# Longformer attention and squared-ReLU expert on one core: batch 1's global rows by one-hot matmuls, and expert matmuls placed ahead of the last scatter

## The chip, the cores and the metric

The kernel runs on one core of one Trainium2 chip. The metric is the device time of one execution in microseconds (us); lower is better. The profile page describes one profiled execution of the same program. Its span is about 2 us shorter than the time of that execution, so spans are compared with spans and times with times.

Every comparison below is a ratio to the kernel before, measured in the same rounds on the same chip, or a distance between two events inside one trace. Where absolute times of different runs are compared all the same, the text says so.

## The reference, cut to what matters

```python
# q, k, v: 8 batches x 8 heads x 576 tokens x 64; global_idx: 8 sorted token numbers
scores = np.matmul(q, k.transpose(0, 1, 3, 2)) / np.sqrt(D)
mask = np.abs(pos[:, None] - pos[None, :]) <= 32              # a window of 65
mask = mask | is_global[:, None] | is_global[None, :]         # 8 global tokens
attn = softmax(np.where(mask, scores, -1e9))
x = np.matmul(attn, v)          # -> (4608 tokens, 512)
h = x @ w_in                    # 512 -> 2048
out = np.square(np.maximum(h, 0)) @ w_out                     # -> (4608, 512) float32
```

The eight global tokens attend to everything and are attended to by everything. So their q, k and v rows are needed beside the windowed ones, and their results must be put into their columns of x ("scatter").

## The kernel before

The kernel works on pairs of heads: pair `i` is batch `i // 4`, heads `2*(i % 4)` and the next. Pairs 0 to 3 are batch 0, pairs 4 to 7 are batch 1. Attention runs on all engines: TensorE (PE) for scores and values, ScalarE (ACT) for exponentials, VectorE (DVE) for casts, copies and normalising, GpSimd (POOL) for the scatter. The expert's matmuls are "fills": blocks that are put between the attention steps to keep PE busy. `mm1` is the first expert matmul (`w_in`), `mm2` the output matmul (`w_out`). A score group covers half of a pair's tokens.

The names in the traces: `stk`, `stq`, `stv` are loaded rows of k, q, v; `natk`, `natq`, `vt` the same in fp16; `kt`, `qt` the transposed ones; `sc` the scores, `et` their exponentials, `acc` the sums of values, `xT` the attention's result, `gx` that of the global tokens; `rl` and `gt` are the expert's relu and its square; `gst` holds gathered rows, `gscr` is the scratch tensor in HBM. `sc`, `acc`, `tr` and `mm` are the buffers in PSUM that this kernel's matmuls write.

Batch 0 picks its global rows with one-hot matmuls (`oh`, `ohp`). All later batches get them by an indirect DMA (gather), a store to a scratch tensor in HBM, and small DMAs from there:

```python
bufs_of = {"sc": 1, "acc": 1, "tr": 1, "mm": 3}       # PSUM buffers by tag

def fetch_globals(b, hp):                              # per pair: 4 + 1 small DMAs
    for nm in "kq":
        js = range(TJ) if b == 1 else (TJ - 1,)
        for h in range(2):
            dst = st[nm][TP : TP + NG, 2 * hp + h, js[0] : TJ]
            nc.sync.dma_start(out=dst, in_=rows(nm)[:, h].unsqueeze(1).to_broadcast(...))
    nc.sync.dma_start(out=st["v"][0:NG, ...], in_=rows("v")...)

def transposed(nm, i):
    nat = nats.pop((nm, i))
    tr = pst("tr" if b else "mm", [P, 1024], FP16)     # k and q of b > 0 share one buffer
    for j in range(TJ):
        n = TP + NG if (b and j == TJ - 1) else TP
        nc.tensor.transpose(tr[:, TP * j : TP * j + n], nat[0:n, j, :], identity[0:n, 0:n])
    if b == 0:                                          # one-hot pick of the global rows
        gl = tr.bitcast(FP32)[:, 384 : 384 + NG]
        for j in range(TJ):
            nc.tensor.matmul(gl, nat[0:TP, j, :], ohp[0:TP, j, :], ...)
```

The part around batch 0's end and batch 1's start, in program order (`...` marks cuts):

```python
    for i in range(4): pool.dma_start(out=w_in[...], ...)     # 4 x 512 KB
    gs0 = gather_rows(0)                                       # POOL: 3 indirect DMAs
    for i in range(NHP):                                       # batch 0, first half
        et = scores(i, 0); ...; pv(*prev); keep_warm(1)
    pv(*prev)
    scatter(0, 0)                                              # 8 POOL copies of 4 pairs
    gather_store(0, gs0)
    ...                                                        # k, q, v of pair 4, its globals
    for j in range(4): pool.dma_start(out=w_out[...], ...)
    for i in range(NHP):                                       # batch 0, second half
        et = scores(i, 1)
        if i == 0: keep_warm(5)                                # idle matmuls
        if prev is not None: pv(*prev)
        fill(2 * step + 1, 2.5)
    pv(*prev); scatter(0, 1); gs1 = gather_rows(1); ...
    casts(NHP, 0); casts(NHP, 1, nc.vector.tensor_copy)        # natk, natq, values of pair 4
    take(2)                                                    # two expert blocks
    tr_k(NHP)
    while fills[0][0] < 16: take(1)
    tr_q(NHP)
    et0 = scores(NHP, 0)                                       # first scores of batch 1
```

`keep_warm(n)` is n matmuls of zeros whose result nobody reads. In `pv`, `acc` has a single buffer, which comes free when `xT` has been written from it.

The softmax here doesn't subtract the row's maximum and nothing guards it: scores larger than these inputs give would overflow.

## Time and profile before

The time before was 373.61 us (median of 3, 373.07 to 373.63).

| What | Value | View |
|---|---|---|
| PE busy | 347.7 of 370.9 us (94%) | page, busy times |
| First expert matmul | 28.91 us | timeline |
| PE waits for batch 1's first k, then q | 3.29 and 1.86 us | timeline |
| First scores of batch 1 | 49.54 us | timeline |
| First output matmul (w_out) | 60.87 us | timeline |
| First expert matmul behind batch 1's last scatter | 89.23 us | timeline |
| Granted clock (share of PE's full clock) 0.50 | 44 to 53.9 us | stretches |

The page of the kernel before: busy times, and the span in 40 slices of 9.3 us with PE's busy share and its granted clock in tenths (9 is 90% or more).

```profile
span 370.9 us, 8149 instructions
PE 347.7 (94%) x2878; PEld 184.8 (50%) x2878; DVE 249.2 (67%) x649; ACT 248.8 (67%) x479; POOL 54.0 (15%) x141
PE   7779689997999999999999999999999999999995
PEclk9978859999999999999999999999999999999999
```

PE is nearly full from the seventh slice on, apart from the tenth. What is to be won lies in the first 60 us.

The timeline of the kernel before. Columns: start and duration in us, engine, source line, operation, output<-inputs, shape, count; in brackets the idle time of that engine ahead of it and what ended it.

```profile
28.91 1.52 PE L475 MATMUL mm<-xT,w_in 128*128 128x256 f16 x8 [0.48 <-POOL xT L646]
42.97 0.56 DVE L386 CAST natk<-stk 104x768 f16<-104x768 f32 x1 [3.10 <-DMA stk<-gscr_k_691]
43.59 0.67 PE L415 MATMUL tr<-identity,natk 96*128 96x96 f16 x6 [3.29 <-DVE natk L386]
45.11 0.56 DVE L394 CAST vt_82<-stv 128x512 f16<-128x512 f32 x2 [1.58 <-DMA stv<-gscr_v_695]
46.78 0.65 DVE L431 COPY kt_72<-tr 128x480 f16<-128x480 f16 x1
47.83 0.65 PE L415 MATMUL tr<-identity,natq 96*128 96x96 f16 x6 [1.86 <-DVE kt_72 L438]
49.54 0.58 PE L557 MATMUL sc<-qt_77,kt_72 64*128 64x160 f16 x10 [0.31 <-DVE qt_77 L450]
50.05 3.60 PE L475 MATMUL mm<-xT,w_in 128*128 128x256 f16 x16
60.87 1.03 PE L496 MATMUL mm<-w_out,gt 128*128 128x512 f16 x4
```

Read it backwards from the first scores of batch 1 (49.54): they waited for qt, qt for the q transpose (47.83), that for the copies out of the one `tr` buffer (46.78). These copies stood in DVE's queue behind the cast of v at 45.11, for which DVE had waited 1.58 us, until the gathered rows of v (`gscr_v`) had landed. The train begins with the cast of natk at 42.97, which DVE did at once when the gathered rows of k (`gscr_k`) had landed. The gather had been issued at 21.97 us, so 21 us lie between it and the cast.

The same stretch as busy times of the kernel before. Columns: stretch, length, then for PE, weight loads, DVE, ACT, POOL the busy us (instructions), then granted clock, DMA share, GB/s.

```profile
40.00:42.00 2.00, 0.30 (x3) 0.02 (x1) 0.00 (x0) 0.00 (x0) 0.46 (x3) 1.00 1.01 136
44.00:46.00 2.00, 1.96 (x12) 1.11 (x9) 0.61 (x3) 1.41 (x3) 1.70 (x2) 0.50 1.24 208
```

After PE had stood still for 3.29 us, its granted clock was 0.50 until 53.9 us: the 16 expert matmuls at 50.05 took 3.60 us, and the 16 at 55.01, at a granted clock of 1.00, took 1.92 us.

### The profile page before, as it was taken

Reading aid. Unit: us, or ns where it says so; the run is one execution under the profiler, and the core shown is the slowest. Engines: PE = TensorE matmul, PEld = TensorE weight load, DVE = VectorE, ACT = ScalarE, POOL = GpSimd, SP = SyncE. Lnnn points to the kernel's source line nnn. Section 1 sums busy time; section 2 is a strip of 40 time slices with the busy share of each in tenths; the row PEclk is TensorE's granted clock in tenths of the full one; section 3 lists DMA queues with packets and bytes.
Section 4 is the critical chain, followed back from the end, with each engine's and each line's share of the span. In section 5 each row is a group of like instructions: output and inputs, shape, how many; then the busy total and the mean of one; then the engine's idle time right before and its main releaser. Section 6 shows DMA issues by size and latency. Waiting matters only on the chain.

```text
span 370.9 us, 8149 instructions
## 1 busy us (share of the span) xinstructions
PE 347.7 (94%) x2878; PEld 184.8 (50%) x2878; DVE 249.2 (67%) x649; ACT 248.8 (67%) x479; POOL 54.0 (15%) x141
## 2 busy tenths in 40 slices
PE   7779689997999999999999999999999999999995
PEld 3546456553545555555555555555555544444442
DVE  7652447566788988788878887888788863422421
ACT  6656336565997799769976997699769952612610
POOL 5375520004200340020002000200020001000000
PEclk9978859999999999999999999999999999999999
DMA  8899997769774574355435633562010002002002
GB/s 204 181 153 197 174 224 166 169 159 222 194 188 129 129 191 118 97 156 160 100 97 157 159 101 97 156 160 67 30 60 29 2 28 85 1 28 85 2 31 82
DMA packets 65650, 44.22 MB, mean 119 GB/s; under 512 B 43114, under 2 KB 60618, under 8 KB 65610
## 3 DMA queue, kind: packets, MB, share of 16 engines
q1 hardware_dynamic: 60200, 38.14, 39.8%
q0 software_dynamic: 4992, 4.98, 8.0%
q10 hardware_dynamic: 418, 0.59, 0.6%
q8 instruction: 22, 0.36, 0.4%
q14 instruction: 18, 0.15, 0.1%
HBM read 38.06 MB, written 9.83 MB: 129 GB/s over the span
## 4 chain that ended last, share of the span: by engine, by line
PE 59%; issue 15%; DMA 9%; DVE 6%; ACT 5%; POOL 3%; POOLq 1%; SPq 1%; ACTq 0%; DVEq 0%
PE mm L496 25%; PE mm L460 23%; DMA stv<-in_v_dram 4%; PE acc L595 4%; PE tr L415 3%; PE sc L557 3%; DMA gstq<-in_q_dram,gidx 3%; ACT rl L465 2%; DMA gstk<-in_k_dram,gidx 2%; DVE gt L466 2%; ACT er L563 1%; POOL xT L646 1%; POOLq L637 1%; DVE et L567 1%; ACT natq L386 1%
## 5 line engine op out<-in xcount | busy, mean ns | idle before, releaser
L496 PE MATMUL mm<-w_out,gt 128*128 128x512 f16 x576 | 133.7, 379 | 0.0
L460 PE MATMUL mm<-xT,w_in 128*128 128x512 f16 x512 | 119.0, 379 | 1.0 <-POOL xT L646 1.0
L465 ACT ACTIVATE rl<-mm 128x512 f16<-128x512 f32 x128 | 72.1, 594 | 33.0 <-PE mm L460 32.2
L496 PEld LDWEIGHTS <-gt 128*128 128x128 f16 x576 | 53.3, 97 | 55.4
L460 PEld LDWEIGHTS <-w_in 128*128 128x128 f16 x512 | 47.3, 97 | 50.3 <-issue 1.3
L605 ACT ACTIVATE rec<-acc 64x288 f32<-64x288 f32 (+1 forms) x112 | 45.4, 405 | 32.0 <-PE acc L595 25.5
L618 DVE TENSOR_TENSOR xT<-acc,rec 64x288 f16<-64x288 f32 (+1 forms) x112 | 50.8, 454 | 19.2 <-ACT rec L606 17.9
L466 DVE TENSOR_TENSOR gt<-rl 128x512 f16<-128x512 f16 x128 | 50.1, 421 | 16.6 <-ACT rl L465 15.8
L646 POOL COPY xT<-gx 128x4 f16 x72 | 19.8, 275 | 228.7 <-DVE xT L618 220.5
L563 ACT ACTIVATE er<-sc 128x912 f16<-128x912 f32 (+1 forms) x48 | 44.0, 916 | 5.5 <-PE sc L557 5.0
L567 DVE TENSOR_TENSOR et<-er,mask 128x912 f16<-128x912 f16 (+1 forms) x48 | 29.9, 622 | 21.3 <-ACT er L563 20.9
L502 DVE COPY ot<-mm 128x512 f32<-128x512 f32 x36 | 24.9, 691 | 26.0 <-PE mm L496 25.3
L386 ACT CAST natq<-stq 104x768 f16<-104x768 f32 (+1 forms) x32 | 26.4, 825 | 9.4 <-DMA stv<-gscr_v_695 5.2
L606 ACT ACTIVATE rec<-rec 128x288 f32<-128x288 f32 x64 | 28.3, 443 | 2.0
L563 ACT ACTIVATE et<-sc 128x912 f16<-128x912 f32 (+1 forms) x16 | 14.6, 913 | 14.5 <-PE sc L557 14.3
L386 DVE CAST natk<-stk 104x768 f16<-104x768 f32 (+1 forms) x32 | 17.8, 555 | 3.4 <-DMA stk<-gscr_k_691 3.1
L475 PE MATMUL mm<-xT,w_in 128*128 128x256 f16 x128 | 18.6, 306 | 0.5 <-POOL xT L646 0.5
L415 PE MATMUL tr<-identity,natk 96*128 96x96 f16 x168 | 12.4, 212 | 4.6 <-DVE natk L386 4.5
L415 PE MATMUL tr<-identity,natq 96*128 96x96 f16 x168 | 12.4, 211 | 3.6 <-DVE kt_72 L438 2.1
L475 PEld LDWEIGHTS <-w_in 128*128 128x128 f16 x128 | 13.3, 109 | 4.3 <-issue 1.0
L610 DVE TENSOR_REDUCE gs<-acc 128x16 f32<-128x32 f32 x32 | 6.0, 187 | 11.9 <-ACT rec L605 11.9
L415 PEld LDWEIGHTS <-natq 96*128 96x128 f16 x192 | 9.3, 99 | 9.1 <-issue 2.6
(195 smaller groups left out, 317.6 us busy)
## 6 DMA issues: line engine op xcount, KB each, us to landing
stk<-in_k_dram SPq DMA_DIRECT2D x32, 288.0 KB
out_dram<-ot SPq DMA_DIRECT2D x36, 256.0 KB
stq<-in_q_dram SPq DMA_DIRECT2D x30, 288.0 KB
stv<-in_v_dram SPq DMA_DIRECT2D x64, 120.0 KB
w_in<-in_moe_w_in_dram POOLq DMA_DIRECT2D x4, 512.0 KB, 9.0
w_out<-in_moe_w_out_dram POOLq DMA_DIRECT2D x4, 512.0 KB, 9.3
stv<-in_v_dram SPq DMA_DIRECT2D x32, 48.0 KB
stq<-in_q_dram ACTq DMA_DIRECT2D x2, 288.0 KB
```

The lines of the kernel that those rows point to most:

```text
L386: op(out=nat[0:n].rearrange("p j (h d) -> p h j d", d=D), in_=st[nm][0:n, 2 * hp : 2 * hp + 2],)
L415: nc.tensor.transpose(tr[:, TP * j : TP * j + n], nat[0:n, j, :], identity[0:n, 0:n])
L460: nc.tensor.matmul(ph, w_in[:, t, u * P : (u + 1) * P], xT[:, t, XOFF + c * TC : XOFF + (c + 1) * TC], start=(t == 0), stop=(t == NDM - 1),)
L465: nc.scalar.activation(out=rl, in_=ph, func=AF.Relu)
L466: nc.vector.tensor_tensor(out=gts[c][:, u, :], in0=rl, in1=rl, op=ALU.mult)
L475: nc.tensor.matmul(ph[:, j], w_in[:, t, (u + j) * P : (u + j + 1) * P], xT[:, t, half * (256 + XOFF) : half * (256 + XOFF) + 256], start=( ...
L496: nc.tensor.matmul(po, gts[c][:, f, m * P : (m + 1) * P], w_out[:, f, :], start=(f == 0), stop=(f == NFF - 1),)
L563: nc.scalar.activation(out=er[:, :, 0:W], in_=sc[:, :, 0:W], func=AF.Exp, bias=0.0, scale=scale)
L567: nc.vector.tensor_tensor(out=et[:, :, 0:W], in0=er[:, :, 0:W], in1=mask[:, MB[half] : MB[half] + W].unsqueeze(1).to_broadcast((P, 2, W)), ...
L605: nc.scalar.activation(out=rec[r], in_=av[rs, xs, :, 0:GTOK], func=AF.Ln)
L606: nc.scalar.activation(out=rec, in_=rec, func=AF.Exp, scale=-1.0)
L618: nc.vector.tensor_tensor(out=xT[r, hp, x0 : x0 + HS].rearrange("p (k x) -> p k x", k=2), in0=av[r, x, :, 0:GTOK], in1=rec[r], op=ALU.mult,)
```

## The change

It has two parts. The first takes batch 1's global rows by one-hot matmuls, as batch 0 does, so that no DMA of gathered rows stands before batch 1. The second scatters three of four pairs ahead of the last one, and runs three of the four k-tiles of three expert blocks while the last pair is normalised. The diff, cut to its core:

```diff
 # part 1: picks instead of gathered rows for batch 1
-            js = range(TJ) if b == 1 else (TJ - 1,)
+            js = range(TJ) if b == 2 else (TJ - 1,)
-        n = TP + NG if b else TP
+        n = TP + NG if b > 1 else TP
-        tr = pst("tr" if b else "mm", [P, 1024], FP16)
+        tr = pst("mm" if b == 0 or (nm == "q" and i <= 2 * NHP) else "tr", [P, 1024], FP16)
-        if b == 0:
+        if b < 2:
-    gs0 = gather_rows(0)
-    gather_store(0, gs0)
-    fetch_globals(1, 0)
-    pool.tensor_copy(out=w_out[0:1, 0, 0:1], in_=st["k"][...])
+    pool.tensor_copy(out=w_out[0:1, 0, 0:1], in_=w_in[32:33, 0, dff - 1 : dff])
     tr_q(NHP)                    # and behind tr_q of pairs 5, 6, 7
+    v_globals(NHP)
 # part 2: early scatter, early expert matmuls
+    scatter(0, 0, slice(0, NHP - 1))
     pv(*prev)
-    scatter(0, 0)
+    et = scores(0, 1)
+    for u in range(0, 6, 2):
+        mm1_half(u, 0, range(NDM - 1))
+    scatter(0, 0, slice(NHP - 1, NHP))
+    for u in range(0, 6, 2):
+        fills.pop(0)
+        mm1_half(u, 0, range(NDM - 1, NDM))
-        if i == 0:
-            keep_warm(5)
-        fill(2 * step + 1, 2.5)
+        fill(2 * step + 1, 2 if i else 0)
 # in pv: the globals are normalised ahead of xT, for every batch
+        if half == 0 and (hp == NHP - 1 or (b == 0 and hp == NHP - 2)):
+            ...                       # reciprocal, multiply -> gxs[b]
         for r, x, rs, xs in parts:
             nc.vector.tensor_tensor(out=xT[...], in0=av[...], in1=rec[r], op=ALU.mult)
-        if half == 0 and hp == NHP - 1:
-            ...                       # reciprocal, multiply
 # further, not shown: a trigger for w_in, pair 3's value cast moved and its picks' copy on DVE
```

The result is the same.

More of the change, by code (lines that the diff above doesn't have):

```diff
@@ L394, in cast_values, with v_globals @@
             op(out=vts[i % NBUF][0:n, tsl, 0:3:2], in_=st["v"][0:n, tsl, hs])
-    def v_globals0(i):
-        vs = vts[i][:, :, 0:3:2]
+    def v_globals(i):
+        vs = vts[i % NBUF][:, :, 0:3:2]
         gl = pst("mm", [P, 512])[0:NG, 0 : 2 * D]
@@ L401, in v_globals0 @@
         gvs = sbt("gvs", [NG, 2 * D], FP16, bufs=2)
-        nc.scalar.copy(out=gvs, in_=gl)
+        (nc.vector.tensor_copy if i == NHP - 1 else nc.scalar.copy)(out=gvs, in_=gl)
         nc.vector.tensor_copy(
@@ L411, in transposed @@
         b = i // NHP
-        tr = pst("tr" if b else "mm", [P, 1024], FP16)
+        tr = pst("mm" if b == 0 or (nm == "q" and i <= 2 * NHP) else "tr", [P, 1024], FP16)
         for j in range(TJ):
-            n = TP + NG if (b and j == TJ - 1) else TP
+            n = TP + NG if (b > 1 and j == TJ - 1) else TP
             nc.tensor.transpose(
@@ L466, in mm1, with mm1_half @@
         nc.vector.tensor_tensor(out=gts[c][:, u, :], in0=rl, in1=rl, op=ALU.mult)
-    def mm1_half(u, half):
+    ph_now = {}
+    def mm1_half(u, half, tiles=range(NDM)):
         if 0 not in gts:
             gts[0] = sbt("gt", [P, NFF, TC], FP16, bufs=2)
-        ph = pst("mm", [P, 2, 256])
+        if 0 in tiles:
+            ph_now[u] = pst("mm", [P, 2, 256])
+        ph = ph_now[u]
         for j in range(2):
-            for t in range(NDM):
+            for t in tiles:
                 nc.tensor.matmul(
@@ L477, in mm1_half @@
                     xT[:, t, half * (256 + XOFF) : half * (256 + XOFF) + 256],
-                    start=(t == 0), stop=(t == NDM - 1), skip_group_check=True,
+                    start=(t == 0 and j == 0), stop=(t == NDM - 1), skip_group_check=True,
                 )
+        if NDM - 1 not in tiles:
+            return
         rl = sbt("rl", [P, TC], FP16, bufs=3).rearrange("p (j x) -> p j x", j=2)
@@ L540 @@
     gsum = {}
+    gxs = {}
     def scores(i, half):
@@ L613, in pv @@
             )
+        if half == 0 and (hp == NHP - 1 or (b == 0 and hp == NHP - 2)):
+            gs = gsum[b]
+            a, z = (0, NHP) if b else (0, NHP - 1) if hp < NHP - 1 else (NHP - 1, NHP)
+            gr = sbt("gr", [P, NHP, NG], FP32, bufs=2)
+            if a == 0:
+                gxs[b] = sbt("gx", [P, NHP, NG], FP16, bufs=2)
+            for r, x, rs, xs in parts:
+                nc.vector.reciprocal(out=gr[r, a:z], in_=gs[rs, a:z, xs])
+            for r, x, rs, xs in parts:
+                nc.vector.tensor_tensor(
+                    out=gxs[b][r, a:z], in0=gs[r, a:z, x], in1=gr[r, a:z], op=ALU.mult
+                )
         x0 = b * S + half * HS
@@ L621, in pv @@
             )
-        if half == 0 and hp == NHP - 1:
-            gs = gsum[b]
-            gr = sbt("gr", [P, NHP, NG], FP32, bufs=2)
-            gsum[b] = sbt("gx", [P, NHP, NG], FP16, bufs=2)
-            for r, x, rs, xs in parts:
-                nc.vector.reciprocal(out=gr[r], in_=gs[rs, :, xs])
-            for r, x, rs, xs in parts:
-                nc.vector.tensor_tensor(out=gsum[b][r], in0=gs[r, :, x], in1=gr[r], op=ALU.mult)
     gvs = {}
@@ L639, in load_columns, with scatter @@
         )
-    def scatter(b, part=None):
+    def scatter(b, part=None, pairs=slice(0, NHP)):
         lo, hi = {
@@ L646, in scatter @@
             nc.gpsimd.tensor_copy(
-                out=xT[:, :, lo:hi][:, :, ds(gvs[part][g], 1)],
-                in_=gsum[b][:, :, g : g + 1],
+                out=xT[:, pairs, lo:hi][:, :, ds(gvs[part][g], 1)],
+                in_=gxs[b][:, pairs, g : g + 1],
             )
@@ L689 @@
         clear_values(pool.memset, vt)
-    pool.tensor_copy(out=w_in[0:1, 0, 0:1], in_=st["v"][32:33, 0, H - 2, D - 1 : D])
+    pool.tensor_copy(out=w_in[0:1, 0, 0:1], in_=st["k"][32:33, H - 1, TJ - 1, D - 1 : D])
     for i in range(4):
         pool.dma_start(out=w_in[:, :, ts(i, 512)], in_=wv[:, :, ts(i, 512)])
-    gs0 = gather_rows(0)
     prev = None
@@ L702 @@
             tr_q(i + 1)
-        if i == NHP - 1:
-            cast_values(nc.vector.tensor_copy, i)
-        v_globals0(i)
+        v_globals(i)
+        if i == NHP - 2:
+            cast_values(nc.vector.tensor_copy, i + 1)
         if prev is not None:
@@ L735 @@
     fetch_pair(1, 0)
-    fetch_globals(1, 0)
-    pool.tensor_copy(out=w_out[0:1, 0, 0:1], in_=st["k"][32:33, 1, TJ - 1, D - 1 : D])
+    pool.tensor_copy(out=w_out[0:1, 0, 0:1], in_=w_in[32:33, 0, dff - 1 : dff])
     for j in range(4):
@@ L743 @@
         fetch_pair(1, hp)
-        fetch_globals(1, hp)
     step = 4
@@ L749 @@
     for i in range(NHP):
-        et = scores(i, 1)
-        if i == 0:
-            keep_warm(5)
+        if i:
+            et = scores(i, 1)
         if prev is not None:
             pv(*prev)
-        fill(2 * step + 1, 2.5)
+        fill(2 * step + 1, 2 if i else 0)
         prev = (i, 1, et)
@@ L784 @@
     tr_q(NHP + 1)
+    v_globals(NHP + 1)
     prev = None
@@ L793 @@
             (tr_k, tr_q)[half](i + 1)
+            if half and i + 1 < 2 * NHP:
+                v_globals(i + 1)
             take(2)
```

## The prediction

> **What bounds the kernel now.** By the page, TensorE (PE) is busy 347.7 of 370.9 us; by stretches, over 99% from 120 to 300 us. What can be won is before 60 us. Three losses (timeline, PE's waits, stretches):
> 1. The first expert matmul starts at 28.91 us, when the scatter of the globals' columns (8 POOL copies, 26.82 to 28.86) is through; 2.31 us of idle matmuls fill the gap.
> 2. PE stands still from 40.3 to 43.6 us: batch 1's first k transpose waits for natk's cast, that for the DMA of the gathered globals (stk<-gscr_k). ACT waits for stv<-gscr_v to 44.6, DVE (in order) reaches the kt copies at 46.8, and PE waits 1.9 us more because the q transpose shares the one "tr" buffer.
> 3. The granted clock is 0.50 from 23.2 to 29.9 and from 43.6 to 53.9 us. [...]
>
> **Removed.** For batch 1: 20 small DMAs, a gather with three stores on POOL, their waits; five idle matmuls; q's share of "tr".
>
> **Added.** Per pair of batch 1: 12 one-hot matmuls for k and q (0.27 us per 6 in batch 0), 5 for v (0.38), an ACT copy (0.25), a DVE copy (0.33): 0.92 us of PE, 3.7 over four pairs. Eight more POOL copies, about 2 us, beside other work.
>
> **Moved.** 18 matmuls (0.21 us each, cold) run while the last pair is normalised and scattered. w_in starts about 0.7 us earlier, w_out 2 to 3; w_out should finish about 44 instead of 49 us, before its first use.
>
> **Steps.**
> - At about 31 us the kernel before has one expert block and two score groups done; I expect three blocks and one group. That is about 2 us ahead, but one block was only done later, under the wait.
> - k, q, v of batch 1's first pair land by about 38 us, so natk runs at once. Next bound is DVE in order: xT, natk, v casts, squares, kt, qt. Batch 1's scores start about 44.7 instead of 49.5 us: **4.8 us won**, PE still idle about 2.5 us before it.
> - Then the same work, cold as before or warm: 0 to 1.7 us won.
> - The picks of pairs 5 to 7 lie on full PE: **2.8 us lost**. The wait for "tr" goes: up to 0.5 won.
> - From batch 1's scatter (86 us) on nothing changes.
>
> Net 2 to 4.5 us: **predicted 370.0 us** (-1.0%), range 367.0 to 372.7. Faster by over 2%: 0.06; within 2%: 0.92; slower: 0.02.
>
> **What would show it.** First output matmul (w_out, gt) at 54 to 56 instead of 60.9 us; no wait on gscr before it; first batch 1 scores at 44 to 45.5 with DVE's qt copy as releaser; the partial expert matmuls at 25.5 to 27; between the first output matmul and batch 2 about 2.5 us more than before; from there to the end the same length within 1 us.
>
> **What would make it wrong.** Clock: full speed over 40 to 46 us gives up to 2 us more; a cold window more in 23 to 34 takes 1 to 2. If w_out slows the pair's load past 41 us, the gain shrinks. The q and v picks in the three "mm" buffers may make output groups wait (about 1 us per pair). If DVE's order binds less, scores start at 43 and the gain is 6.

4.8 + (0 to 1.7) - 2.8 + (0 to 0.5) gives 2.0 to 4.2 us, put down as "net 2 to 4.5". "Cold" means half clock. What the forecast gives for the clock (0 to 1.7, up to 2, and 1 to 2 us) are estimates whose origin it doesn't state; by the trace of the kernel before, 16 expert matmuls took 1.68 us longer at 0.50 than at 1.00 (3.60 and 1.92 us), and the 24 early ones took 4.27 us in the changed kernel (granted clock 0.64) and 2.94 in after_again (1.00).

## The result, and the profile after

The changed kernel took 369.9 us (median of 4, 368.85 to 370.36), against 373.62 us for the kernel before in the same measurement (4 runs, 373.07 to 374.86). The ratio is 0.9892, with a 95% interval of 0.9858 to 0.9926. Ratios here are the mean time of one kernel's fast runs over that of the other's of the same rounds, so not quite the ratio of the medians. Measured again on another chip, with 5 rounds, it was 0.9895 (0.9857 to 0.9934).

The page of the changed kernel, the same lines:

```profile
span 368.4 us, 8258 instructions
PE 347.7 (94%) x2941; PEld 186.0 (51%) x2941; DVE 250.5 (68%) x656; ACT 249.2 (68%) x482; POOL 51.3 (14%) x143
PE   7779799988899999999999999999999989999995
PEclk9978999998999999999999999999999999999999
```

PE's busy time is the same to 0.1 us although 63 matmuls were added, because fewer of them ran at half clock: the 8 and 5 of slices five and six of its granted clock are now 9. But there is a new 8 in the tenth slice: from 84 to 86 us the granted clock was 0.54.

The timeline of the changed kernel:

```profile
26.46 4.27 PE L479 MATMUL mm<-xT,w_in 128*128 128x256 f16 x24 [0.64 <-POOL xT L658]
40.42 0.55 DVE L386 CAST natk<-stk 96x768 f16<-96x768 f32 x1
41.02 0.43 PE L415 MATMUL tr<-identity,natk 96*128 96x96 f16 x6
42.76 0.65 DVE L431 COPY kt_72<-tr 128x480 f16<-128x480 f16 x1
43.60 0.75 DVE L446 COPY qt_77<-mm 128x576 f16<-128x576 f16 x1
44.49 0.40 PE L564 MATMUL sc<-qt_77,kt_72 64*128 64x160 f16 x10 [1.65 <-DVE qt_77 L450]
44.83 1.92 PE L479 MATMUL mm<-xT,w_in 128*128 128x256 f16 x16
53.81 1.03 PE L502 MATMUL mm<-w_out,gt 128*128 128x512 f16 x4
```

natk no longer waits for any DMA: DVE takes it in its turn. The first scores start at 44.49 instead of 49.54 us, and the expert matmuls behind them take 1.92 us at a granted clock of 1.00.

The later part, in PE's timeline: first the two lines of the kernel before (behind batch 1's last scatter; the last value accumulation of batch 7), then those of the changed kernel.

```profile
89.23 1.89 PE L460 MATMUL mm<-xT,w_in 128*128 128x512 f16 x8 [0.99 <-POOL xT L646]
304.21 0.54 PE L595 MATMUL acc<-et,vt_79 128*128 128x112 f16 x6 [0.69 <-DVE xT L618]
```

```profile
84.19 3.54 PE L460 MATMUL mm<-xT,w_in 128*128 128x512 f16 x8 [0.99 <-POOL xT L658]
301.91 0.54 PE L602 MATMUL acc<-et,vt_79 128*128 128x112 f16 x6 [1.60 <-DVE xT L638]
```

With these events the 2.5 us of the two spans (370.9 and 368.4) split without a remainder:

| Stretch | Before | After | Gain |
|---|---|---|---|
| start to first scores of batch 1 | 49.54 | 44.49 | +5.05 |
| to the first output matmul | 11.33 | 9.32 | +2.01 |
| to the first expert matmul behind batch 1's last scatter | 28.36 | 30.38 | -2.02 |
| to the end | 281.67 | 284.21 | -2.54 |
| sum | 370.90 | 368.40 | +2.50 |

So 7.06 us were won by the first output matmul, and 4.56 us were given back in this execution. The third row is steady: 30.37 to 30.39 us in all nine profiles with picks for pairs 5 to 7, 28.36 in all three with gathered rows for the whole batch. The second row varies: three later profiles whose code up to there is the same have 10.58 (after_again), 10.44 (gx_late) and 10.27 us (warm_gap) instead of 9.32; the granted clock was 1.00 there too, as far as it was read (to 52 us). In after_again PE waits 0.86 us there for `xT`, which it doesn't in the first profile; the runs don't show why. The profiled execution of the changed kernel was the slowest of the four; they took 370.36, 370.25, 369.55 and 368.85 us at a mean granted clock of 0.985, 0.989, 0.991 and 0.994. So part of what is given back comes and goes with the clock.

### The profile page after: what moved, and what is told of

Read it like the earlier page. It is cut to its first block, busy times and chain, and to the rows that moved or that the text cites. A ratio compares the mean times of both kernels' runs of the same rounds, so it can differ in the third digit from the quotient of the medians.

```text
span 368.4 us, 8258 instructions
## 1 busy us (share of the span) xinstructions
PE 347.7 (94%) x2941; PEld 186.0 (51%) x2941; DVE 250.5 (68%) x656; ACT 249.2 (68%) x482; POOL 51.3 (14%) x143
## 4 chain that ended last, share of the span: by engine, by line
PE 60%; issue 14%; DVE 7%; DMA 6%; ACT 5%; POOL 4%; POOLq 2%; ACTq 0%; SPq 0%; DVEq 0%
PE mm L502 25%; PE mm L460 24%; PE acc L602 4%; PE tr L415 3%; DMA w_in<-in_moe_w_in_dram 3%; PE sc L564 3%; DVE gt L466 2%; DMA stq<-in_q_dram 2%; POOLq L649 2%; ACT rl L465 2%; DMA stv<-in_v_dram 1%; POOL xT L658 1%; ACT er L570 1%; ACT natq L386 1%; DVE et L574 1%
## 5 line engine op out<-in xcount | busy, mean ns | idle before, releaser
L460 PE MATMUL mm<-xT,w_in 128*128 128x512 f16 x512 | 120.7, 382 | 1.0 <-POOL xT L658 1.0
L466 DVE TENSOR_TENSOR gt<-rl 128x512 f16<-128x512 f16 x128 | 50.2, 421 | 18.2 <-ACT rl L465 17.5
L658 POOL COPY xT<-gx 128x4 f16 (+2 forms) x80 | 21.8, 272 | 231.1 <-DVE xT L638 226.8
L479 PE MATMUL mm<-xT,w_in 128*128 128x256 f16 x128 | 16.8, 290 | 0.6 <-POOL xT L658 0.6
L491 DVE TENSOR_TENSOR gt<-rl 128x512 f16<-128x512 f16 x16 | 6.8, 426 | 8.4 <-ACT rl L490 8.1
```

The source lines that it names most:

```text
L460: nc.tensor.matmul(ph, w_in[:, t, u * P : (u + 1) * P], xT[:, t, XOFF + c * TC : XOFF + (c + 1) * TC], start=(t == 0), stop=(t == NDM - 1),)
L466: nc.vector.tensor_tensor(out=gts[c][:, u, :], in0=rl, in1=rl, op=ALU.mult)
L479: nc.tensor.matmul(ph[:, j], w_in[:, t, (u + j) * P : (u + j + 1) * P], xT[:, t, half * (256 + XOFF) : half * (256 + XOFF) + 256], start=( ...
```

## The experiments

My theory: the gain is the removed wait for gathered rows together with the clock that this wait had cost; the picks of pairs 5 to 7 cost PE 2 us; and the last 2.5 us are a half-clock stretch (1.65 us) and the new order in `pv` (0.9 us). The rivals were that the early scatter and early expert matmuls bring the gain, that the clock is worth nothing, and that the picks are free.

Twelve kernels ran. All outputs are right. "Changed" is the kernel after the change.

| Label | Edit | Ratio to before (95%) |
|---|---|---|
| picks_only | part 1 alone | 0.9861 (0.9816 to 0.9906) |
| early_only | part 2 alone | 1.0001 (0.9956 to 1.0046) |
| before_warm | before + idle matmuls in the wait | 0.9963 (0.9905 to 1.0020) |
| hybrid | changed, gathered rows for pairs 5 to 7 | 0.9960 (0.9905 to 1.0015) |
| after_again | changed | 0.9895 (0.9857 to 0.9934) |
| gx_late | changed, old order in pv | 0.9847 (0.9806 to 0.9888) |
| warm_gap | changed + 6 idle matmuls | 0.9856 (0.9819 to 0.9892) |
| dve_first | changed, one draining later | 0.9852 (0.9816 to 0.9887) |
| combo | changed + the last three edits | 0.9831 (0.9798 to 0.9863) |
| picks_tuned | part 1 + warm_gap + dve_first | 0.9895 (0.9863 to 0.9928) |
| combo_warm | combo + 4 idle matmuls | 0.9825 (0.9793 to 0.9857) |
| combo_hybrid | combo, gathered rows for pairs 5 to 7 | 0.9946 (0.9913 to 0.9980) |

The first four shared one chip, the next four a second, the last four a third. In the last group one execution of the kernel before took 581 us; it was not counted.

### Which part brings the gain: picks_only and early_only

```diff
 # picks_only: the kernel before, with part 1 of the diff above and nothing of part 2
 # early_only: the changed kernel, with part 1 undone:
-        if b < 2:
+        if b == 0:
+    gs0 = gather_rows(0)             # behind the issue of w_in
+    gather_store(0, gs0)
+    fetch_globals(1, 0)              # and of pairs 5, 6, 7
```

> The kernel before with only batch 1's one-hot picks (no gather for batch 1, no DMA of its globals); scatter, idle matmuls and fills as before. My theory (the gain is the wait for the gathered globals): batch 1's first scores at 44 to 45 us, first output matmul at 54 to 55.5, time within 1 us of the changed kernel, about 370 to 371 us. Rival (the early scatter and early expert matmuls bring most of it): less than half of the gain is here, time above 372 us.

> The changed kernel with batch 1's globals back on gather and DMA; split scatter and early expert matmuls kept. My theory: three expert blocks are done by about 31 us, but the wait on the globals' DMA still ends at about 43 us, the first output matmul stays at 60 to 61 us, time 373 to 374.5 us, the same as before or slightly more. Rival: first output matmul 2 us or more earlier, time below 372 us.

PE's timeline of picks_only:

```profile
45.57 0.40 PE L557 MATMUL sc<-qt,kt 64*128 64x160 f16 x10 [1.15 <-DVE qt L450]
55.78 1.03 PE L496 MATMUL mm<-w_out,gt 128*128 128x512 f16 x4
```

DVE's, then PE's timeline of early_only:

```profile
44.02 0.56 DVE L386 CAST natk<-stk 104x768 f16<-104x768 f32 x1 [1.04 <-DMA stk<-gscr_k]
```

```profile
49.61 0.65 PE L415 MATMUL tr<-identity,natq 96*128 96x96 f16 x6 [4.54 <-DVE kt L438]
51.19 0.58 PE L564 MATMUL sc<-qt,kt 64*128 64x160 f16 x10 [0.17 <-DVE qt L450]
62.80 1.03 PE L502 MATMUL mm<-w_out,gt 128*128 128x512 f16 x4
```

Part 1 alone gives a gain that can't be told from the whole one: 0.9861, against 0.9892 and 0.9895 for the changed kernel on other chips. Its marks came a little later than expected (45.57 for 44 to 45 us, 55.78 for 54 to 55.5 us).

Part 2 alone gives nothing: natk still comes at 44.02 us, behind the gathered rows, and what was done early is only waited for later. The expected first output matmul of early_only was missed by 2 us (62.80). The profiled execution was the slowest of its five (380.07 us, median 376.61), and it was late already at the first scores of batch 0's second half: 27.75 us, against 25.64 us in the kernel before. From those scores to the first output matmul early_only takes 35.05 us and the kernel before 35.23. The rival falls, as far as the changed kernel goes.

Part 1 also takes q's transposes of batch 1 out of the one `tr` buffer, and no run separates this from the wait for gathered rows. In the trace of the kernel before its effect looks small: the q transpose had ended at 48.48 us, and the square that stood ahead of the qt copy in DVE's queue ended only at 48.74.

### What the clock is worth: before_warm

```diff
     take(2)
+    keep_warm(15, "acc")             # zeros into the free acc buffer
     tr_k(NHP)
     while fills[0][0] < 16: take(1)
+    keep_warm(7, "acc")
     tr_q(NHP)
```

> The kernel before with 15 + 7 more idle matmuls where TensorE waits in 40 to 48 us; all waits kept, only the clock can change. If the half clock of 43.6 to 53.9 us is a part of the gain: clock 1.0 there, first output matmul about 1.7 to 2.5 us earlier (58.4 to 59.2 us), time about 371.5. If the clock is worth nothing (all is wait): within 0.5 us of before.

PE's timeline of before_warm:

```profile
50.30 0.40 PE L557 MATMUL sc<-qt,kt 64*128 64x160 f16 x10 [1.25 <-DVE qt L450]
59.61 1.03 PE L496 MATMUL mm<-w_out,gt 128*128 128x512 f16 x4
```

All waits are kept, and the granted clock is 1.00 from 42 to 60 us. From the first scores to the first output matmul it takes 9.31 us, against 11.33 in the kernel before and 9.32 in the changed one. So of the 7.06 us of the two profiles, 2.0 are the clock. The other 5.05 are not: from the cast of natk (43.51) to the first scores before_warm takes 6.79 us and the kernel before 6.57, so the full clock doesn't shorten that train. They go with the removed waits: in the changed kernel natk's cast comes 2.55 us earlier (40.42 instead of 42.97), and from it to the scores it takes 4.07 us; picks_only, with part 1 alone, has 4.46. The absolute time expected (58.4 to 59.2) was missed by 0.4 us, for this execution was later before: its first scores of batch 1 came at 50.30 instead of 49.54. In the whole time the ratio is 0.9963 and its interval reaches 1: with 3 rounds and half clock elsewhere in some executions (in the profiled one at 88 us, where 8 expert matmuls took 3.31 instead of 1.89 us and the page has an 8 for the granted clock), a gain of 2 us isn't clear of noise, so this verdict rests on the trace.

### What the picks of pairs 5 to 7 cost, and what the other way costs: hybrid and combo_hybrid

```diff
-        if b < 2:
+        if i <= NHP:                 # picks for pair 4 only
+    gs0 = gather_rows(0)             # hybrid: behind the early scatter, ahead of w_out;
+                                     # combo_hybrid: behind the issue of w_out
+    gather_store(0, gs0)             # behind scatter(0, 1)
+    for hp in range(1, NHP):         # moved here from ahead of the second half
+        fetch_pair(1, hp)
+        fetch_globals(1, hp)
```

> The changed kernel, but only the first pair of batch 1 takes its globals by one-hot matmuls; the other three by gather and DMA again, with the gather put behind the early scatter. If the picks of pairs 5 to 7 cost 2 us on a full TensorE: first output matmul at about 54 us as in the changed kernel, and 28.4 us instead of 30.4 from there to batch 1's last scatter; time about 368 us. If they cost nothing (hidden): same as the changed kernel, 370 us. A new wait on gathered globals before pair 5's k transpose would show as DVE natk late.

> The combined kernel with the picks for pair 4 alone and a gather for pairs 5 to 7 that is issued behind w_out, so that w_out is not delayed as in the hybrid before. If that delay was what cost: w_out's gate at about 46 us, no wait of natk on the gathered globals, 2 us faster than the combined kernel. If the extra small DMAs themselves slow the loads of the pairs: natk waits for DMA again at 58 to 64 us and it is slower than the combined kernel by 1 us or more.

Combo_hybrid was slower than combo in the same rounds (0.9946 and 0.9831). Hybrid has 0.9960; its partner, the changed kernel, ran on other chips (0.9892 and 0.9895), and the intervals overlap a little. Its expectations were missed: the first output matmul came at 55.03 us, and from there to batch 1's last scatter it took 33.64 us, not 28.4. In hybrid the gathers also delayed w_out: its third quarter had landed at 49.14 instead of 45.60 us. In combo_hybrid that fault is gone (45.90 us), and the rows still come too late. DVE's timeline of combo_hybrid, the casts of pairs 5 and 6:

```profile
54.58 0.56 DVE L386 CAST natk<-stk 104x768 f16<-104x768 f32 x1 [2.22 <-DMA stk<-gscr_k]
61.59 0.56 DVE L386 CAST natk<-stk 104x768 f16<-104x768 f32 x1 [1.43 <-DMA stk<-gscr_k]
```

The DMA queue of combo_hybrid shows why the second is late too. These are the issues of k of pair 5, of pair 5's global rows, and of k of pairs 6 and 7:

```profile
46.54 0.40 SPq L102 DMA_DIRECT2D stk<-in_k_dram  x1
...
52.66 0.63 SPq L128 DMA_DIRECT2D stk<-gscr_k  x2
...
54.44 0.32 SPq L102 DMA_DIRECT2D stk<-in_k_dram  x1
...
59.64 0.32 SPq L102 DMA_DIRECT2D stk<-in_k_dram  x1
```

In the changed kernel the same three loads of k are issued at 46.25, 50.21 and 53.33 us. So a pair takes 6.5 instead of 3.5 us of the queue. Not all of that is the small DMAs: of the first interval, 2.7 us (49.92 to 52.66) are a wait of the queue until the store of the gathered rows of k had landed (POOL's next gather, released by the same store, follows at 52.90). Hybrid has no such wait there, and its intervals are 6.27 and 4.90 us.

From the first output matmul (51.97) to the first expert matmul behind the last scatter (87.42) combo_hybrid takes 35.45 us, combo and the changed kernel 30.38 each. PE waits 3.8 us for natk in it, and behind these two waits runs 16 output matmuls slowly, in 3.38 and 3.28 us per eight instead of 1.89 (I take it for half clock; the granted clock wasn't read there). The picks cost 2.02 us of that stretch, as counted; the DMAs cost more. That they could be made free by issuing the gather much earlier stays untried.

### The 2.5 us at the end: after_again, gx_late and warm_gap

```diff
 # gx_late, in pv: the globals ahead of xT for batch 0 only
+        if want and b == 0: norm_globals()
         for r, x, rs, xs in parts: ...         # xT
+        if want and b: norm_globals()
 # warm_gap, in the loop over batches 2 to 7
             et = scores(i, half)
+            if i == 2 * NHP and half == 0:
+                keep_warm(6)
             if i + 1 < B * NHP: ...            # the k transpose of the next pair
```

> The changed kernel again, as the reference of this call: ratio to before 0.985 to 0.992. The profiled run shows whether the half clock at batch 1's last scatter (8 expert matmuls in 3.54 instead of 1.89 us) is there in every execution.

> The changed kernel, with the globals of batches 1 to 7 normalised after xT again, as before the change (batch 0 as changed). My theory: the last value accumulation of batch 7 waits 0.7 us for xT instead of 1.6, the stretch from batch 6's to batch 7's scatter is 34.4 instead of 35.4 us, the kernel 0.9 us faster than the changed kernel. Rival (the tail's 2.5 us is the clock alone): no difference over 0.3 us.

> The changed kernel with 6 idle matmuls (about 1.3 us) in the 1.5 us that TensorE waits for natk before batch 2. If the half clock after it comes from that idle stretch: the 8 expert matmuls after the scatter take 1.9 us in the profiled run and the mean is 0.5 to 1.5 us under the changed kernel. If it comes from elsewhere or is rare: same within 0.4 us.

What PE waits for in the last stretch (from 290 us), first in after_again, then in gx_late. Columns: who waited for whom, us in total, times, longest.

```profile
PE acc L602 <- DVE xT L638: 1.6, 1, 1.6
```

```profile
PE acc L602 <- DVE xT L640: 0.7, 1, 0.7
```

The wait falls by 0.9 us, and the distance from batch 6's scatter to batch 7's from 35.37 us (after_again, 272.31 to 307.68) to 34.44 (gx_late, 272.96 to 307.40), as expected. That is the new order in `pv`: for batches 2 to 7, whose normalising is four DVE instructions on 64 partitions, it stands ahead of the xT that frees `acc`. In the batches before, fills cover it; at the end nothing does.

PE's timeline of warm_gap, the idle matmuls and what follows the scatter:

```profile
80.26 1.47 PE L226 MATMUL tr<-idle 128*128 128x512 f16 x6
...
84.12 1.89 PE L460 MATMUL mm<-xT,w_in 128*128 128x512 f16 x8 [1.00 <-POOL xT L658]
```

With the gap filled the eight expert matmuls take 1.89 us again, at a granted clock of 1.00 (84 to 88 us), and the mean of all executions is 1.7 us under after_again (371.1 and 372.8 us). In the profiled executions of after_again, gx_late and dve_first, where the gap is open, they took 3.18, 3.57 and 3.40 us, at 0.68, 0.54 and 0.57 over 84 to 88 us. But it isn't certain with an open gap: the kernel before, picks_only and hybrid had 1.89 us with nearly the same idle stretch (1.24, 1.36 and 1.49 us). All five kernels in which the gap is filled (warm_gap, combo, combo_warm, picks_tuned, combo_hybrid) have 1.89. The half clock there isn't owed to the change: before_warm, which from there on is the kernel before, took 3.31 us. The means of gx_late and warm_gap lie about 1.6 us under after_again, but the intervals overlap; the sizes that I hold to are those in the traces.

### What sets the start of batch 1: dve_first

```diff
+    hold[0] = 14                     # block 14: matmuls now, relu and square later
     take(2)
     tr_k(NHP)
     ...
     v_globals(NHP)
+    drain_half(hold[0][0], 0, hold[0][1])
```

> The changed kernel, with the draining (relu and square on VectorE, 1.1 us) of expert block 14 put behind the copies of kt and qt of batch 1's first pair. If VectorE's order sets the start of batch 1's scores: they start about 1 us earlier relative to the cast natk (3.1 instead of 4.1 us after it starts), and the kernel is 0.7 to 1 us faster. Rival (TensorE's own order sets it): no change.

Timelines of after_again, then of dve_first: the cast of natk and the first scores of batch 1.

```profile
41.15 0.55 DVE L386 CAST natk<-stk 96x768 f16<-96x768 f32 x1
45.23 0.40 PE L564 MATMUL sc<-qt,kt 64*128 64x160 f16 x10 [1.65 <-DVE qt L450]
```

```profile
39.93 0.55 DVE L386 CAST natk<-stk 96x768 f16<-96x768 f32 x1
42.94 0.40 PE L572 MATMUL sc<-qt,kt 64*128 64x160 f16 x10 [0.57 <-DVE qt L450]
```

From the cast to the scores it takes 3.01 instead of 4.08 us. The 1.1 us that were moved behind the copies match the 1.07 us won here, so DVE's order sets this start, not PE's. Not all of it is kept: from the cast to the first output matmul dve_first takes 14.02 us (to 53.95) and after_again 14.66 (to 55.81), for PE then waits 1.35 instead of 0.86 us for `xT`. The first profile of the changed kernel took only 13.39. The ratios (0.9852 and 0.9895) point to a gain, and their intervals overlap.

### All together: combo, combo_warm and picks_tuned

```diff
 # combo: gx_late, warm_gap and dve_first at once
 # picks_tuned: picks_only with warm_gap and dve_first (the old order in pv is in it)
 # combo_warm: combo, and
     scatter(0, 0, slice(0, NHP - 1))
+    keep_warm(4)
     pv(*prev)
```

> The changed kernel with the three edits at once (late normalising, idle matmuls in the gap, later draining of block 14). If their effects add (0.9 + about 1.5 + 1.1 us): ratio to before 0.976 to 0.982, about 3 us under the changed kernel. If they share one cause: no better than the best of them, 0.985.

> The one-hot picks alone, with the idle matmuls in the gap and the later draining (the late normalising is in it already): the combined kernel without the early scatter and early expert matmuls. If the early part is worth one expert block once nothing else hides it: 0.7 to 1 us slower than the combined kernel. If it is worth nothing: equal within 0.3 us.

> The combined kernel with 4 idle matmuls in the 1.3 us wait before batch 0's last value accumulation (about 23 us). If that wait causes the half clock in 26 to 30 us: the 24 early expert matmuls take 2.9 us instead of 4.3 in every execution and the kernel is 0.3 to 1 us faster than the combined one. Where the clock is still half at 23 us the idle matmuls take 1.7 us and cost 0.4 us. Most likely within 0.5 us of the combined kernel.

Combo took 369.05 us against 376.46 for the kernel before on the same chip: 0.9831, short of the range that I gave for full adding (0.976 to 0.982), and lower than each edit alone (0.9847 to 0.9856 on another chip; the intervals overlap). Combo_warm is the same within noise (368.66 us, 0.9825) and is the fastest kernel found; it beats both kernels, by 1.75% and, comparing ratios across chips, by about 0.7% (their intervals just touch). Its 24 early matmuls took 2.94 us, but combo's took 3.00 without the idle matmuls, so its own question has no answer here. Its 1.7 us for four idle matmuls at half clock was an estimate of mine; in the kernel before, five took 2.31 us at 0.50.

Picks_tuned was a miss of mine in a useful way. I expected part 2 to be worth 0.7 to 1 us once nothing hides it; picks_tuned was 2.3 us slower than combo (371.34 and 369.05 us). PE's timelines, first of combo, then of picks_tuned: the first scores of batch 0's second half, the first expert matmuls, the first output matmul.

```profile
25.92 0.36 PE L572 MATMUL sc<-qt,kt 64*128 64x112 f16 x6
26.90 3.00 PE L479 MATMUL mm<-xT,w_in 128*128 128x256 f16 x24 [0.62 <-POOL xT L671]
...
53.56 1.03 PE L510 MATMUL mm<-w_out,gt 128*128 128x512 f16 x4
```

```profile
25.25 0.36 PE L565 MATMUL sc<-qt,kt 64*128 64x112 f16 x6
...
28.90 1.17 PE L475 MATMUL mm<-xT,w_in 128*128 128x256 f16 x8 [2.10 <-POOL xT L654]
...
55.23 1.03 PE L504 MATMUL mm<-w_out,gt 128*128 128x512 f16 x4
```

From those scores to the first output matmul combo takes 27.64 us and picks_tuned 29.98. Picks_tuned waits 2.10 us for the whole scatter before its first expert matmul, and five idle matmuls bridge only 1.25 us of the rest at a granted clock of 1.00 (2.31 us at 0.50 in the kernel before). So part 2, with the small further changes, has a worth of its own, which in early_only was hidden behind the gathered rows.

How large it is depends on the clock. Up to batch 1's first scores the profiled picks_tuned has a mean granted clock of 0.91 and combo 1.00, so the 2.3 us are early work and clock together. At like clock the traces show less from the first scores of batch 0's second half to the first scores of batch 1: 18.94 us in picks_tuned and 17.57 in combo_hybrid (0.91 and 0.92), 19.96 in picks_only and 19.03 in the changed kernel (0.91 both). By these, the early work is worth about 0.9 to 1.4 us (an estimate), not far from what I had expected. Five of the ten profiles with part 2 have a granted clock of 1.00 in that stretch, none of the four without; whether part 2 is the reason isn't settled.

In the whole time of the changed kernel part 2 is not seen: picks_only is at 0.9861 and the changed kernel at 0.9895, on different chips and not apart by their intervals. The order in `pv` takes back 0.9 us of it; the rest isn't accounted for.

## Why the prediction was right

The time was predicted at 370.0 us and measured at 369.9. The chance of 0.92 for "within 2%" was well placed. That the hit is so close is partly luck: the gains before the first output matmul were put too low, and a loss of 2.54 us behind it was left out, so the errors cancel in part. And the gain of the two profiled executions is 2.50 us, that of the medians 3.7.

- **Batch 1's start: right.** 44.7 us predicted, 44.49 measured, with DVE's copy of qt as releaser and no DMA ahead of natk. dve_first confirms that DVE's order is the bound. The idle time of PE before it was 1.65 us, not 2.5.
- **"Cold as before or warm: 0 to 1.7 us won": too small.** It was warm (granted clock 1.00 from 44 to 54 us), and worth 2.0 us in the first profile (11.33 to 9.32 us; before_warm has 9.31), less in the later ones (10.27 to 10.58). The first output matmul came at 53.81, just ahead of the 54 to 56 predicted.
- **The picks of pairs 5 to 7: right in kind.** 2.8 us lost less up to 0.5 for the `tr` wait was predicted; 2.02 us were measured between the first output matmul and batch 2.
- **"From batch 1's scatter on nothing changes": wrong.** The rest took 2.54 us longer, of which 1.65 is a half-clock stretch at 84 us (3.54 instead of 1.89 us) and 0.91 the wait for `acc` in batch 7 (1.60 instead of 0.69). The first is a risk that I had named only for 23 to 34 us; before_warm has it without the change. The second stands in the diff: four DVE instructions were put ahead of xT for every batch, and I had looked at batch 0 alone.
- **Three blocks and one score group at about 31 us: right** (the 24 matmuls end at 30.73 us). "w_in starts about 0.7 us earlier" was wrong: 18.57 against 18.49 us. Its trigger ran earlier, but POOL then idled 2.10 us ahead of the issue, for which the profile names nothing; no run tests what that cost. w_out was issued 2.0 us earlier, as predicted (33.30 against 35.31), but its third quarter had landed at 45.60 instead of 47.09 us, a smaller gain than the 5 us foreseen.

As a sum: predicted 4.8 + (0 to 1.7) - 2.8 + (0 to 0.5) - 0; in the profiled spans 5.05 + 2.01 - 2.02 - 2.54 = 2.50. The medians differ by 3.7 us, since the profiled execution of the changed kernel was its slowest and that of the kernel before its fastest.

What set the clock isn't shown. The half clock from 43.6 us came behind 3.29 us of idle PE and lasted 10.3 us (granted clock 0.50); that from 23.2 us set in within an idle stretch of only 1.15 us (see the last section). No run shows the cause of the spread between executions of one kernel. DVE's order counts by the traces: in the kernel before the copies of kt came only at 46.78 us, behind the cast of v, though their transposes had ended at 44.26. dve_first shows what such an order costs here: 1.1 us of relu and square ahead of the copies delayed PE by 1.07 us.

## What to carry to other kernels

When a stage waits for data that came the long way (gather, store, small loads), picking it with matmuls from tiles that are on the chip anyway can be cheaper even at a cost in PE time: here 2 us of PE against 5 us of wait and up to 2 us of clock. Value a gain from the wait that ends last: the same early work was worth nothing while the gathered rows ended later, and about 1 to 2 us, part of it clock, when they no longer did. And if an edit changes an order inside a helper, follow it through all of its callers: the reorder that served batch 0 cost 0.9 us in batch 7.

## What the traces show of the clock and the small DMAs

- The clock was also halved after stretches that were not idle: in the changed kernel PE was busy 1.70 us of the 4 us up to 84 us, with matmuls in between, and the granted clock fell to 0.54; with 3.03 us busy of about the same 4 us (warm_gap) it stayed at 1.00. In the kernel before, 1.70 us busy in the 4 us up to 89 us left it at 1.00. Short idle stretches came ahead of it too: 1.15 us at the half clock of 23.2 us (kernel before), and 2.20 and 1.59 us ahead of the slow matmuls of combo_hybrid (3.38 and 3.28 us per eight). These runs don't settle a share of busy time, or a length of idle time, at which it happens.
- The twelve stores of 32 KB took 3.3 to 5.3 us from issue to landing and the gathers of 128 rows 4.8 to 5.4 (medians), by the table of DMA issues of the kernel before. These runs don't show load as the reason for the differences: a store took 3.4 us at a DMA share of 0.82 (33.70 to 37.10 us) and another 5.3 at 0.87 (132.46 to 137.76 us).
- Each of the five small DMAs per pair held its issuing queue for about 0.26 to 0.34 us, and a pair took 4.9 to 6.3 us of the queue (hybrid) instead of 3.1 to 4.0 (changed kernel).
